# Thirteen tiles of v read as float by SyncE, and the second projection of two more groups by Strassen

## The chip, the core and the metric

The kernel runs on one core of a Trainium2 chip. A core has five engines with a queue of their own each: TensorE (PE: products; PEld: the weight load that precedes each), VectorE (DVE), ScalarE (ACT), GpSimd (POOL) and SyncE (SP), which here only issues DMAs. Sixteen DMA engines carry all transfers. The metric is the device time of one execution in microseconds.

## What is computed

Inputs q, k, v have the shape (4, 8, 768, 64): batch, heads, positions, head size. A recurrence over positions with a decay per head is followed by two projections with a sine activation between them.

```
gamma = 1.0 - 2.0 ** (-5.0 - np.arange(H, dtype=np.float32))
scale = 1.0 / np.sqrt(D)
for t in range(S):
    state = gamma[None, :, None, None] * state + np.einsum('bhd,bhe->bhde', k[:, :, t], v[:, :, t])
    y[:, :, t] = scale * np.einsum('bhd,bhde->bhe', q[:, :, t], state)
...
h = x @ w_in
s = np.sin(alpha * h)
g = h + s * s / (alpha + 1e-09)
return (g @ w_out).astype(np.float32)
```

x is y with the heads side by side: 3072 tokens of 512. w_in is 512 by 2048, w_out 2048 by 512, alpha has 2048 values.

## The kernel before

**Tiles and groups.** The 24 tiles of 128 tokens are taken in the order `P` (`order`): tiles 0 to 3 are the first of each batch, then come batch 0, batch 1, and batches 2 and 3 interleaved. A number n below means `P[n]`. Ten groups of 4, 2, 2, 2, 2, 2, 2, 2, 2 and 4 tiles pass through the projections: group 5 has tiles 12 and 13, group 6 tiles 14 and 15, group 7 tiles 16 and 17, group 8 tiles 18 and 19, group 9 tiles 20 to 23.

**Order of work.** The schedule is written by hand: each engine executes its instructions in the order in which the program emits them. `PLAN` is the order up to group 1. From group 2 on `phase(g, ...)` (L878) runs slots: a slot of a two-tile group makes two of the 16 blocks f of the hidden layer. It issues 8 products into `ph` (L610), the sine and the square on ScalarE (L613, L618), what is hung on the slot (`atts`: bursts of the recurrence, transposes, scalings), then its share of the second projection of the group before (`outs`), then `add` (L625, VectorE), which writes block f of `gT` and frees ph's bank of PSUM. What is in `behind_slot` comes last. "(7,1)" is slot 1 of group 7. Four banks of PSUM have the tag mm; ph and the outputs of the second projection share them.

**The second projection** of a group has 32 products of 512 columns for two tiles (`ff_out`, L634), with one copy per tile to SBUF on VectorE (L644) and one store by SyncE (L647). For the groups in `fast`, 8 and 9, it goes by Strassen (`Seven`): seven sums of eight products of 256 columns for each pair of tiles. Products 3 and 4 take blocks of gT as they are; products 5 and 2 take the sums "s", 7 and 6 the differences "d" and 1 the sums "x", which `mix_g` (L687) forms, in three operations for a slot's blocks, mostly on GpSimd (L710). The products' right sides are blocks of w_out or of sums of them, which `mix_w` forms (L675, L681): seven of ten pieces of 1024 elements on GpSimd, three on VectorE. `hold` copies product 5 and 2's bank b to SBUF, `cross`, `rest` and `main` (VectorE) make the outputs from banks a and c.

**Reads.** Tiles 0 to 10 are read one by one (`load_chunk`, into `qkr` and `vr`). The other 13 (batch 1's tiles 11 to 13, five of batch 2 and five of batch 3) are read "wide" by `load_seq` (L131, issue in L149): one DMA for each of the eight heads brings several tiles. All these are issued by GpSimd, and convert from float to bf16 on the way. GpSimd's queue has, after `PLAN`, q, k and v of batch 1, q, k and v of batch 2 and the first two tiles of batch 3's q and k, one directly behind the other; v and the other three tiles of batch 3 follow at (5,5) (`last_loads`). v is then multiplied in place by a table of decays (`scale_v`, L185): tiles 9 to 14 on VectorE at (2,3) to (4,6), the later ones on GpSimd. q and k are transposed by SyncE's DMA (`turn`, L297), each tile two bursts ahead; SyncE's queue holds these and the stores of the outputs in one order.

**Buffers that matter.** `gT` has one tag with two buffers of the largest size, 16 KB per partition, whatever the size of the group. `vr` has 11 buffers, `qkr` 10. w_mix lies in five buffers of qkr, in `dec` and in batch 1's `qk_seq1` once these are free; g_mix of group 8 in five of qkr, of group 9 in `qk_seq2` and `qk_seq3`.

Of the kernel before, what the change touches and what calls it, by code (L numbers as in the profile page):

```python
# [8 lines left out]
F32 = mybir.dt.float32  # L9
# [29 lines left out]
def kernel(  # L39
# [90 lines left out]

    def load_seq(bt, names="qkv", part=slice(None), between=None):  # L131
# [8 lines left out]
        fs = slice(2 * (now[0] - cs[0]), 2 * (now[-1] - cs[0]) + 2)  # L140
        for name, src in (("q", q), ("k", k), ("v", v)):
            if name not in names:
                continue
            for n, (b, m, e) in enumerate(heads):
                if n == 3 and between is not None:
                    scale_v(between, nc.gpsimd)
                r, at = half(b), 2 * m + e
                o = tv[r, fs, at, :] if name == "v" else tqk[r, fs, "qk".index(name), at, :]
                nc.gpsimd.dma_start(out=o, in_=src[bt, head(b, m, e), now[0] * C:(now[-1] + 1) * C, :].rearrange("(f i) d -> i f d", i=64))  # L149
# [35 lines left out]
    def scale_v(j, eng):  # L185
        t, by = raw["v", j], kg
        if wide(j):
            t, by = t.rearrange("i f p d -> i (f p) d"), kgq
        eng.tensor_mul(t, t, by[:, j % NCH, :, None].to_broadcast([128, H, D]))  # L189

# [405 lines left out]
    class Slot:  # L596


        def __init__(self, g, f, cols=None, nf=1, tag="mm"):
# [3 lines left out]
            if g not in gT:  # L603
                gT[g] = work.tile([128, FF, n], BF16, name="gT", tag="gT", bufs=2)
            w = self.hi - self.lo
# [46 lines left out]

    fast = (8, 9)
    FH, NH = FF // 2, d_model // 2
# [4 lines left out]
    def w_block(k, n, js):  # L659
# [3 lines left out]
             6: ((0, 0), (0, 1), ALU.add), 7: ((1, 0), (1, 1), ALU.add)}  # L663
    w_todo = [(n, i) for n in (4, 3, 1, 7, 6) for i in range(2)]

    def w_homes():
        for _ in range(5):
            yield big.tile([128, 4, NH], BF16, name="w_mix", tag="qkr", bufs=10)
        for pool, tag, n in ((consts, "dec", 2), (big, "qk_seq1", 3)):
            t = pool.tile([128, n, 4, NH], BF16, name="w_mix", tag=tag)  # L670
            for i in range(n):
                yield t[:, i]
    w_home = w_homes()

    def mix_w(eng):  # L675

        n, i = w_todo.pop(0)
        a, b, op = W_MIX[n]
        js = slice(4 * i, 4 * i + 4)
        w_mix[n, i] = next(w_home)  # L680
        eng.tensor_tensor(w_mix[n, i], w_block(*a, js), w_block(*b, js), op=op)  # L681

# [37 lines left out]
    class Seven:  # L720
# [20 lines left out]
        def right(self, n, j):  # L741
            if n in (5, 2):
                return w_out[:, j + FH * (n == 5), NH * (n == 5):NH * (n == 5) + NH]
            return w_mix[n, j // 4][:, j % 4]

# [26 lines left out]
        def store_both(self, o, n):  # L772

            t0, t1 = groups[self.g][2 * self.p:2 * self.p + 2]
            if self.g < NG - 1:
                self.store(0, o[:, 0], n)
                self.store(1, o[:, 1], 1 - n)
                return
# [19 lines left out]
        def main(self, which=None):  # L798
# [28 lines left out]
    def fast_pieces(g):  # L827
        J = range(FH)

        def banks(k):  # L830
            if k == "c":
                return psum.tile([128, 2, 512], F32, name="c", tag="pa")[:, 0, 0:NH]
            if "ab" not in po:
                po["ab"] = psum.tile([128, 2, 512], F32, name="ab", tag="two")
            return po["ab"][:, "ab".index(k)].rearrange("p (x n) -> p x n", x=2)
        s = Seven(g, 0, banks)
        return s.pieces((4, J), (3, J), (5, J), (2, J), lambda: s.hold(nc.vector), s.cross, (1, J), s.rest, (7, J), (6, J), s.main)
# [40 lines left out]
    def phase(g, outs, att, nf=1, on_vector=(), tags={}, early=()):  # L878


        no, done = len(outs), 0
        for n in range(FF // nf):
# [162 lines left out]

    load_seq(1, "q", between=P[8])
    load_seq(1, "k")
    load_chunk(P[10], "v")
    load_seq(1, "v")
    load_seq(2, "q")  # L1050
    load_seq(2, "k")
    load_seq(2, "v")
    load_seq(3, "q", slice(0, 2))
    load_seq(3, "k", slice(0, 2))
    for j in P[15:17] + P[18:19]:
        scale_v(j, nc.gpsimd)

# [12 lines left out]
    def B(old, new, first, beside, second):  # L1070

        return lambda: burst(old, new, first, beside=beside, second=second)

    for n in range(9, 17):
# [3 lines left out]
        at(where[n] if n < 16 else (5, 5), X(P[n + 2]))  # L1078
    for i, spot in ((16, (6, 4)), (18, (7, 4)), (20, (8, 1))):
# [6 lines left out]
    for i, spot in ((19, (6, 1)), (20, (6, 5)), (21, (7, 1)), (22, (7, 5)), (23, (8, 0))):  # L1086
        at(spot, X(P[i]))
    for i, spot in ((19, (6, 2)), (20, (6, 6)), (21, (7, 2)), (22, (7, 6)), (23, (8, 2))):
# [12 lines left out]
    for i, spot in ((9, (2, 3)), (10, (3, 0)), (11, (3, 3)), (12, (3, 7)), (13, (4, 3)), (14, (4, 6))):  # L1101
# [45 lines left out]
```

## Time and profile before

| | us |
|---|---|
| median of three runs | 205.69 (205.63 to 206.04) |
| the profiled execution | 207.02 |
| its span on the core | 205.2 |
| granted TensorE clock, mean | 0.997 |

The span runs from the first to the last instruction of the profile. Engine times are busy times; a matmul's end is modelled, so neighbouring rows of TensorE overlap by some tenths, and starts tell the pace. A group row gives operation, shapes, count, busy time, the mean of one and what ended the idle time before it. The chain of waits names, from the last instruction backwards, what each step waited for.

### The profile page before, as it was taken

How to read it: one execution, taken by the hardware profiler on the slowest of the kernel's cores; microseconds unless marked ns; L12 is line 12 of the kernel's file. 1: busy time of each engine (PE TensorE's matmuls, PEld its weight loads, DVE VectorE, ACT ScalarE, POOL GpSimd, SP SyncE). 2: the span in 40 equal slices, each digit the busy share in tenths (PEclk: the TensorE clock that was granted, in tenths of full speed). 3: DMA queues.
4: the chain of work that ended last, by engine and by line, in shares of the span. 5: the costliest groups of instructions: out<-in, count | busy, mean ns of one | idle time of the engine just before them, and what ended most of it. 6: DMA issues, size and time to landing. Idle time of an engine off the chain costs nothing.

```text
span 205.2 us, 6029 instructions
## 1 busy us (share of the span) xinstructions
PE 195.2 (95%) x2426; PEld 131.4 (64%) x2455; DVE 161.5 (79%) x344; ACT 151.8 (74%) x312; POOL 163.2 (80%) x204
## 2 busy tenths in 40 slices
PE   7889999999998999999999999999999999999993
PEld 7444544557765667666666676666766665555983
DVE  5787499877998887887998885995998775577853
ACT  7678888656996877877877959588586869999120
POOL 8998996999999996997399997999193876997000
PEclk9999999999999999999999999999999999999998
DMA  8999999999999999999996796994406101001123
GB/s 133 147 175 192 201 201 176 167 134 106 231 151 188 104 171 194 170 136 150 143 116 117 89 141 117 120 131 104 105 2 107 51 5 51 3 0 51 54 102 102
DMA packets 103580, 24.82 MB, mean 121 GB/s; under 512 B 93392, under 2 KB 101248, under 8 KB 103552
## 3 DMA queue, kind: packets, MB, share of 16 engines
q0 software_dynamic: 80080, 13.38, 92.8%
q1 hardware_dynamic: 23472, 11.06, 26.8%
q8 instruction: 19, 0.31, 0.7%
q14 instruction: 9, 0.07, 0.1%
HBM read 27.30 MB, written 6.29 MB: 164 GB/s over the span
## 4 chain that ended last, share of the span: by engine, by line
PE 83%; DMA 7%; POOL 4%; issue 2%; DVE 2%; ACT 1%; POOLq 0%
PE ph L610 37%; PE po L634 28%; DMA qkT<-qkr 4%; PE a L756 3%; DMA qkr<-in_q_dram 3%; PE ab L756 3%; POOL qkr L125 2%; PE b L756 2%; PE py L373 1%; POOL vr L125 1%; PE c L756 1%; PE pt L291 1%; PE pa L388 1%; PE py L437 1%; POOL w_in L161 1%
## 5 line engine op out<-in xcount | busy, mean ns | idle before, releaser
L625 DVE SCALAR_TENSOR_TENSOR gT<-s,rec_alpha,ph 128x256 bf16<-128x256 f32 (+3 forms) x164 | 79.4, 522 | 25.1 <-ACT s L618 24.6
L610 PE MATMUL ph<-xT,w_in 128*128 128x256 bf16 (+3 forms) x653 | 98.0, 291 | 0.3
L613 ACT ACTIVATE s<-ph,alpha_sb 128x256 f32<-128x256 f32 (+3 forms) x164 | 75.9, 505 | 28.1 <-PE ph L610 26.3
L610 PEld LDWEIGHTS <-w_in 128*128 128x128 bf16 x656 | 63.1, 98 | 29.6 <-DVE s_f L568 0.7
L634 PE MATMUL po<-w_out,gT 128*128 128x512 bf16 x264 | 70.3, 379 | 2.3 <-issue 1.9
L618 ACT ACTIVATE s<-s 128x512 f32<-128x512 f32 (+1 forms) x94 | 58.7, 626 | 2.8
L634 PEld LDWEIGHTS <-gT 128*128 128x128 bf16 x288 | 26.4, 98 | 20.8 <-DVE gT L625 0.5
L710 POOL TENSOR_TENSOR g_mix<-gT 128x512 bf16<-128x512 bf16 (+1 forms) x27 | 25.9, 994 | 7.2 <-DVE gT L625 7.2
L149 POOL DMA_DIRECT2D qk_seq<-in_q_dram x32 | 21.5, 712 | 6.6 <-DMA v_seq<-in_v_dram 6.1
L149 POOL DMA_DIRECT2D qk_seq<-in_k_dram x32 | 21.3, 720 | 1.5 <-DMA qk_seq<-in_q_dram 1.4
L149 POOL DMA_DIRECT2D v_seq<-in_v_dram x24 | 16.8, 743 | 0.0
L681 POOL TENSOR_TENSOR w_mix<-w_out 128x1024 bf16<-128x1024 bf16 x7 | 15.2, 2190 | 0.0
L756 PEld LDWEIGHTS <-g_mix 128*128 128x128 bf16 x128 | 11.9, 98 | 3.6
L644 DVE COPY o_sb<-po 128x512 f32<-128x512 f32 x15 | 10.3, 687 | 2.0 <-PE po L634 1.6
L125 POOL DMA_DIRECT2D vr<-in_v_dram x11 | 10.3, 932 | 1.2 <-DMA w_in<-in_moe_w_in_dram 0.7
L189 POOL TENSOR_TENSOR v_seq<-v_seq,kgq 128x512 bf16<-128x512 bf16 x9 | 9.8, 1097 | 1.4 <-DMA v_seq<-in_v_dram 1.4
L407 DVE TENSOR_TENSOR aTw<-pa,maskq 128x768 bf16<-128x768 f32 x10 | 9.5, 954 | 0.0
L495 DVE TENSOR_TENSOR xT<-py,qg 128x512 bf16<-128x512 f32 x13 | 8.9, 683 | 0.5 <-PE py L453 0.5
L869 PE MATMUL spare<-warm 128*128 128x112 bf16 (+1 forms) x52 | 7.9, 325 | 1.4 <-DVE warm L199 1.2
L391 DVE TENSOR_TENSOR aT<-pa,mask 128x1024 bf16<-128x1024 f32 x7 | 8.5, 1219 | 0.4 <-PE pa L388 0.4
L520 ACT CAST s_q<-s_f 128x256 bf16<-128x256 f32 x13 | 5.1, 393 | 2.7 <-DVE s_f L515 2.7
L165 POOL DMA_DIRECT2D w_out<-in_moe_w_out_dram x8 | 5.8, 727 | 1.2 <-DMA w_in<-in_moe_w_in_dram 0.8
(138 smaller groups left out, 217.7 us busy)
## 6 DMA issues: line engine op xcount, KB each, us to landing
out_dram<-o_sb SPq DMA_DIRECT2D x21, 256.0 KB, 3.9
w_in<-in_moe_w_in_dram POOLq DMA_DIRECT2D x8, 256.0 KB, 8.3
w_out<-in_moe_w_out_dram POOLq DMA_DIRECT2D x8, 256.0 KB, 7.9
vr<-in_v_dram POOLq DMA_DIRECT2D x11, 128.0 KB, 5.3
v_seq<-in_v_dram POOLq DMA_DIRECT2D x16, 80.0 KB, 4.7
qkr<-in_q_dram POOLq DMA_DIRECT2D x7, 128.0 KB, 6.4
qkr<-in_k_dram POOLq DMA_DIRECT2D x7, 128.0 KB, 5.8
qk_seq<-in_q_dram POOLq DMA_DIRECT2D x16, 48.0 KB, 4.4
```

Source lines behind the costliest of these rows:

```text
L125: nc.gpsimd.dma_start(out=t, in_=chunk_of(src, j))
L149: nc.gpsimd.dma_start(out=o, in_=src[bt, head(b, m, e), now[0] * C:(now[-1] + 1) * C, :].rearrange("(f i) d -> i f d", i=64))
L189: eng.tensor_mul(t, t, by[:, j % NCH, :, None].to_broadcast([128, H, D]))
L610: nc.tensor.matmul(self.ph[:, m, :], w_in[:, i, f * 128:(f + 1) * 128], xT[g][:, i, self.lo:self.hi], start=(m == 0 and i == 0), stop=(i = ...
L613: nc.scalar.activation(out=self.s[:, m, :], in_=self.ph[:, m, :], func=ACTF.Sin, scale=alpha_sb[:, f:f + 1])
L618: nc.scalar.activation(out=self.s, in_=self.s, func=ACTF.Square)
L625: nc.vector.scalar_tensor_tensor(gT[self.g][:, f, self.lo:self.hi], self.s[:, m, :], rec_alpha[:, f:f + 1], self.ph[:, m, :], op0=ALU.mult ...
L634: nc.tensor.matmul(po[g, ts], gT[g][:, f, ts * C:(ts + 1) * C], w_out[:, f, :], start=(f == 0), stop=(f == FF - 1))
L644: nc.vector.tensor_copy(o_sb, po[g, ts])
L681: eng.tensor_tensor(w_mix[n, i], w_block(*a, js), w_block(*b, js), op=op)
L710: eng.tensor_tensor(o, i0, i1, op=op)
L756: nc.tensor.matmul(t, self.left(n, j), r, start=k not in self.begun, stop=(j == FH - 1), skip_group_check=True)
```

## The change

In words:
- v of the 13 wide tiles is read by SyncE as float, without conversion, into a new tile `vf` of 16 pieces by 256 values; `scale_v` reads `vf` and writes bf16 into `v_seq`. Batch 1 takes pieces 0 to 5 of `vf`, batch 2 pieces 6 to 15, batch 3 pieces 0 to 9.
- `vf` shares the tag gA, with one buffer, with gT of the four-tile groups 0 and 9. gT of the two-tile groups keeps the tag gT with two, now smaller, buffers.
- `fast` is now 6, 7, 8 and 9. Group 6's pair is laid out over group 7's slots as 4, 5, 2 and hold, 3 and cross, nothing at the pair of the recurrence, 7, half of 6 and 1, the rest; its bank a is of tag mm, b and c of tag two. Group 7's is laid out over group 8's slots with a, b and c of tag mm.
- All w_mix sums are GpSimd's: ten pieces of 512 elements in freed buffers of vr, two of 1024 in dec, three in qk_seq1. g_mix of groups 6, 7 and 8 lies in qkr.
- GpSimd's queue is laid out anew from the end of `PLAN` on: between the wide reads of q and k stand mix_w and the scale_v of tiles 10 to 13, then those of tiles 14 to 18 and 20 at (3,4), (4,0) and (5,3); mix_g of groups 6 and 7 follows in their slots. VectorE keeps the scale_v of tile 9.
- SyncE reads v of batch 1 at (2,2), of batch 2 at (3,3), of batch 3 at (4,6).

```diff
-            for n, (b, m, e) in enumerate(heads):
-                if n == 3 and between is not None:
-                    scale_v(between, nc.gpsimd)
+            if name == "v":
+                vf = raw["vf"][:, 6:16] if bt == 2 else raw["vf"][:, 0:nh]
+                for i, c in enumerate(cs):
+                    raw["vf", bt * NCH + c] = vf[:, 2 * i:2 * i + 2]
+            for n, (b, m, e) in list(enumerate(heads))[some]:
+                if n in between:
+                    between[n]()
...
-                nc.gpsimd.dma_start(out=o, in_=src[bt, head(b, m, e), now[0] * C:(now[-1] + 1) * C, :].rearrange("(f i) d -> i f d", i=64))
+                o = vf[r, fs, at, :] if name == "v" else tqk[r, fs, "qk".index(name), at, :]
+                (nc.sync if name == "v" else nc.gpsimd).dma_start(out=o, in_=src[bt, head(b, m, e), now[0] * C:(now[-1] + 1) * C, :].rearrange("(f i) d -> i f d", i=64))
...
-    fast = (8, 9)
+    fast = (6, 7, 8, 9)
...
+    w_todo = {"vr": [(n, j, 2) for n in (7, 6) for j in range(0, FH, 2)] + [(1, 4, 2), (1, 6, 2)],
+              "dec": [(4, 0, 4), (4, 4, 4)], "seq": [(3, 0, 4), (3, 4, 4), (1, 0, 4)]}
...
+        if g == NG - 3:
+            s = Seven(g, 0, lambda k: psum.tile([128, 2, NH], F32, name=k, tag="mm", bufs=4)[:, slice(0, 2) if k != "c" else 0])
+            parts = [[(4, range(7))], [(4, range(7, FH)), (3, range(6))], [(3, range(6, FH)), (5, range(5))],
+                     [(5, range(5, FH)), (2, range(4))], [(2, range(4, FH)), s.hold], [s.cross, (1, J)], [s.rest, (7, J)],
+                     [(6, J), s.main]]
+            return [s.steps(*p) for p in parts]
+        if g < NG - 3:
...
+            parts = [[(4, J)], [(5, J)], [(2, J), s.hold], [(3, J), s.cross], [], [(7, J)], [(6, range(4)), (1, range(4))],
+                     [(1, range(4, FH)), s.rest, (6, range(4, FH)), s.main]]
+            return [s.steps(*p) for p in parts]
...
+            if g - 1 in fast and n == 5:
+                run(more, "exit1")
...
     def last_loads():
-        mix_w(nc.gpsimd)
         nc.gpsimd.tensor_copy(seen, st["qkT", P[17]][:, 0, 0:1])
-        load_seq(3, "v")
-        mix_w(nc.gpsimd)
-        mix_w(nc.gpsimd)
-        scale_v(P[17], nc.gpsimd)
-        load_seq(3, "qk", slice(2, None))
+        load_seq(3, "q", slice(2, None))
+        load_seq(3, "k", slice(2, None))
...
+    def loads():
+        load_seq(1, "v")
+        turn(P[12])
+        pieces_w(2, "vr")()
+        scale_v(P[10], nc.gpsimd)
+        pieces_w(2, "vr")()
+        load_seq(2, "q")
+        scale_v(P[11], nc.gpsimd)
+        load_seq(2, "k", between={4: scaled(P[12])})
+        scale_v(P[13], nc.gpsimd)
+        load_seq(3, "q", slice(0, 2), between={4: lambda: mix_w(nc.gpsimd, "dec")})
+        mix_w(nc.gpsimd, "dec")
+
+    at((2, 2), loads)
...
+    at((3, 3), lambda: load_seq(2, "v"))
+    at((4, 6), lambda: load_seq(3, "v"))
+    for spot, fn in (((3, 2), pieces_w(2, "vr")), ((3, 2), lambda: load_seq(3, "k", slice(0, 2), some=slice(0, 4))),
+                     ((3, 2), pieces_w(1, "vr")), ((3, 2), lambda: load_seq(3, "k", slice(0, 2), some=slice(4, 8))),
+                     ((3, 4), scaled(P[14], P[15])), ((3, 4), pieces_w(2, "vr")), ((4, 0), scaled(P[16], P[18], P[20])),
+                     ((4, 5), pieces_w(3, "seq")), ((4, 5), pieces_w(1, "vr")), ((5, 3), scaled(P[17]))):
+        mixes(spot, fn)
+    for g in (6, 7, 8):
+        for m in range(0, FH, 2):
+            mixes((g, m + 1), lambda g=g, m=m: mix_g(g, m, 2, nc.gpsimd))
```

More of the change, by code (lines that the diff above doesn't have):

```diff
@@ L140, in load_seq @@
         fs = slice(2 * (now[0] - cs[0]), 2 * (now[-1] - cs[0]) + 2)
+        if "v" in names and "vf" not in raw:
+            raw["vf"] = work.tile([128, 16, NP, D], F32, name="vf", tag="gA", bufs=1)
         for name, src in (("q", q), ("k", k), ("v", v)):
@@ L186, in scale_v @@
         t, by = raw["v", j], kg
+        o = t
         if wide(j):
-            t, by = t.rearrange("i f p d -> i (f p) d"), kgq
-        eng.tensor_mul(t, t, by[:, j % NCH, :, None].to_broadcast([128, H, D]))
+            o, t = (x.rearrange("i f p d -> i (f p) d") for x in (t, raw["vf", j]))
+            by = kgq
+        eng.tensor_mul(o, t, by[:, j % NCH, :, None].to_broadcast([128, H, D]))
     tok = consts.tile([128, NCH, 2], F32, name="tok")
@@ L603, in __init__ @@
             if g not in gT:
-                gT[g] = work.tile([128, FF, n], BF16, name="gT", tag="gT", bufs=2)
+                gT[g] = work.tile([128, FF, n], BF16, name="gT", tag="gA" if sizes[g] == 4 else "gT", bufs=1 if sizes[g] == 4 else 2)
             w = self.hi - self.lo
@@ L663, with mix_w @@
              6: ((0, 0), (0, 1), ALU.add), 7: ((1, 0), (1, 1), ALU.add)}
[L664 to L677, printed above, removed]
-        a, b, op = W_MIX[n]
-        js = slice(4 * i, 4 * i + 4)
-        w_mix[n, i] = next(w_home)
-        eng.tensor_tensor(w_mix[n, i], w_block(*a, js), w_block(*b, js), op=op)
+    w_todo = {"vr": [(n, j, 2) for n in (7, 6) for j in range(0, FH, 2)] + [(1, 4, 2), (1, 6, 2)],
+              "dec": [(4, 0, 4), (4, 4, 4)], "seq": [(3, 0, 4), (3, 4, 4), (1, 0, 4)]}
+    w_home = {}
+    def mix_w(eng, home):
+        n, i, c = w_todo[home].pop(0)
+        a, b, op = W_MIX[n]
+        if home == "vr":
+            to = big.tile([128, 2, NH], BF16, name="w_mix", tag="vr", bufs=11)
+        else:
+            if home not in w_home:
+                w_home[home] = (consts if home == "dec" else big).tile(
+                    [128, 2 if home == "dec" else 3, 4, NH], BF16, name="w_mix", tag="dec" if home == "dec" else "qk_seq1")
+            to = w_home[home][:, (2 if home == "dec" else 3) - 1 - len(w_todo[home])]
+        eng.tensor_tensor(to, w_block(*a, slice(i, i + c)), w_block(*b, slice(i, i + c)), op=op)
+        for j in range(c):
+            w_mix[n, i + j] = to[:, j]
     def blocks(t, first, *dims):
@@ L743, in right @@
                 return w_out[:, j + FH * (n == 5), NH * (n == 5):NH * (n == 5) + NH]
-            return w_mix[n, j // 4][:, j % 4]
+            return w_mix[n, j]
         def mm(self, n, j, half=None):
@@ L810, in main, with steps @@
                 self.store(1, self.o[:, 1, c], 1, c.start, c.stop)
+        def steps(self, *parts):
+            return [fn for part in parts for fn in ([part] if callable(part) else self.pieces(part))]
         def pieces(self, *parts):
@@ L835, in banks, with between @@
             return po["ab"][:, "ab".index(k)].rearrange("p (x n) -> p x n", x=2)
+        if g == NG - 3:
[5 more added lines that the diff above has]
+        if g < NG - 3:
+            def between(k):
+                if k == "a":
+                    return psum.tile([128, 2, NH], F32, name=k, tag="mm", bufs=4)
+                return psum.tile([128, 2, 512], F32, name=k, tag="two")[:, 0].rearrange("p (x n) -> p x n", x=2)[:, slice(0, 2) if k == "b" else 0]
+            s = Seven(g, 0, between)
+            parts = [[(4, J)], [(5, J)], [(2, J), s.hold], [(3, J), s.cross], [], [(7, J)], [(6, range(4)), (1, range(4))],
+                     [(1, range(4, FH)), s.rest, (6, range(4, FH)), s.main]]
+            return [s.steps(*p) for p in parts]
         s = Seven(g, 0, banks)
@@ L878, in phase @@
     def phase(g, outs, att, nf=1, on_vector=(), tags={}, early=()):
-        no, done = len(outs), 0
+        plan = outs if outs and isinstance(outs[0], list) else None
+        no, done = 0 if plan else len(outs), 0
         for n in range(FF // nf):
@@ L901, in phase @@
                 rest[0] = fresh
+            for fn in plan[n] if plan else ():
+                fn()
             while done < min(no, no * (n + 1) * nf // FF):
@@ L1044, with scaled @@
         act(word)
-    load_seq(1, "q", between=P[8])
+    def scaled(*js):
+        return lambda: [scale_v(j, nc.gpsimd) for j in js]
+    load_seq(1, "q", between={3: scaled(P[8])})
     load_seq(1, "k")
     load_chunk(P[10], "v")
[L1049 to L1056, printed above, removed]
     where = {}
@@ L1072, in B, with pieces_w @@
         return lambda: burst(old, new, first, beside=beside, second=second)
+    def pieces_w(n, home):
+        return lambda: [mix_w(nc.gpsimd, home) for _ in range(n)]
     for n in range(9, 17):
@@ L1077 @@
         at(where[n], B(P[n - 1], new, first, P[17] if n == 16 else None, e3 if n == 15 else None))
-        at(where[n] if n < 16 else (5, 5), X(P[n + 2]))
+        if n != 10:
+            at(where[n] if n < 16 else (5, 5), X(P[n + 2]))
     for i, spot in ((16, (6, 4)), (18, (7, 4)), (20, (8, 1))):
```

15 lines of the change are left out of this document (4 added, 11 removed).

## The prediction

> **What bounds the kernel now.** Read first the page's busy shares and its chain that ended last, then the busy time by stage: 62.3 to 122.2 us, then groups 6, 7, 8 and 9.
>
> ```profile
> span 205.2 us, 6029 instructions
> ...
> PE 195.2 (95%) x2426; PEld 131.4 (64%) x2455; DVE 161.5 (79%) x344; ACT 151.8 (74%) x312; POOL 163.2 (80%) x204
> ...
> PE 83%; DMA 7%; POOL 4%; issue 2%; DVE 2%; ACT 1%; POOLq 0%
> ```
>
> ```profile
> 62.30:122.20 59.90, 58.58 (x812) 40.73 (x822) 51.70 (x107) 45.36 (x98) 51.55 (x71) 1.00 1.71 143
> 122.20:137.60 15.40, 15.29 (x207) 10.48 (x208) 13.01 (x29) 12.29 (x27) 13.99 (x20) 1.00 1.33 123
> 137.60:152.90 15.30, 15.19 (x207) 10.52 (x208) 12.04 (x27) 11.75 (x25) 10.77 (x10) 1.00 0.43 77
> 152.90:169.70 16.80, 16.23 (x253) 11.30 (x256) 12.88 (x27) 12.22 (x27) 11.21 (x11) 1.00 0.24 50
> 169.70:189.80 20.10, 20.00 (x121) 11.88 (x122) 13.82 (x21) 19.37 (x33) 17.45 (x19) 1.00 0.08 27
> ```
>
> After span come PE, PEld, DVE, ACT, POOL, clock, DMA share and GB/s. TensorE has 0.1 us idle in all of group 6 and 0.1 in all of group 7. So each product removed in group 7 or 8 is worth its time, and each microsecond that TensorE must wait is paid in full: nothing behind it has slack to give back (group 9 runs TensorE at 20.00 of 20.10 us and ScalarE at 19.37). GpSimd has 1.4 us left in group 6 and 4.5 in group 7, and the change adds to just these.
>
> **What the Strassen pairs remove.** The chain of waits, first in group 6, then at the end, shows the rates:
>
> ```profile
> 134.31 0.87 PE ph L610 x8
> 135.19 0.86 PE po L634 x4
> ...
> 197.70 1.75 PE a L756 x16
> ```
>
> A 512-column output product costs 0.86 / 4 = 0.215 us, a 256-column one 1.75 / 16 = 0.109. A pair now takes 32 of the first, 6.88 us; by Strassen 56 of the second, 6.10. With 0.78 to 0.86 a pair I take 0.86 (proportion to columns: 8 x 0.87 / 8), so groups 6 and 7 together give **-1.7 us**.
>
> The Trainium skill, "TensorE: Matmul & The Clock Gate", section "Back-to-back issue gap", speaks against it: in a stream of weight load and product pairs it has 81 ns for 128 columns and 131 for 512. Estimated from that page, 98 ns for 256 would make a Strassen pair 5.5 us against 4.2, +2.6 us for the two and 208.3 in all; this trace has 0.215 us for 512 columns, not 0.131, and here the measurement decides.
>
> VectorE gets cross, rest and main (three operations) for two copies, and ScalarE one hold:
>
> ```profile
> L644 DVE COPY o_sb<-po 128x512 f32<-128x512 f32 x15 | 10.3, 687 | 2.0 <-PE po L634 1.6 <-ACT o_sb L642 0.4
> L765 ACT COPY b_sb<-b 128x512 f32<-128x512 f32 x2 | 1.2, 585 | 5.2 <-PE b L756 5.2
> ```
>
> That is +0.7 us of VectorE and +0.6 of ScalarE a pair, beside 12.04 and 11.75 of 15.3 us (group 7): hidden by that slack. Of rest and main only main ends a group, where the copy of the second tile stands today. In group 8 two output banks are held out of the four tagged mm, so ph has two. A ph starts at 137.62, and the add of the ph before it, which starts 1.74 earlier, ends at 138.50 + 0.87 = 139.37. So a bank is held for 3.49 us, and two slots are 3.48:
>
> ```profile
> 137.62 1.04 PE L610 MATMUL ph<-xT,w_in 128*128 128x256 bf16 x8
> ...
> 139.36 1.04 PE L610 MATMUL ph<-xT,w_in 128*128 128x256 bf16 x8
> ...
> 145.54 0.42 PE L544 MATMUL y<-qkT,s_q 64*64 64x128 bf16 x16
> ```
> ```profile
> 138.50 0.87 DVE L625 SCALAR_TENSOR_TENSOR gT<-s,rec_alpha,ph 128x256 bf16<-128x256 f32 x2
> ```
>
> So ph is just in time; the bursts between stretch the slots. I take 0, at worst 0.5. At (7,0), that is group 7's slot 0 at 137.62 (y of (7,4) at 145.54 fixes the count), product 4 of group 6 needs block f=15, whose add ends at 138.50 + 0.87 = 139.37, while TensorE is there at 137.62 + 0.87 + 7 x 0.109 = 139.25: **+0.15** with the signal.
>
> **What decides: GpSimd up to (7,1).** There TensorE wants product 5 of group 6 for all eight blocks. Its left side is the sum "s" of g_mix; blocks 6 and 7 come from the last mix_g of group 6, on GpSimd, behind all its earlier work in one queue. TensorE reaches block 6 at 139.36 + 0.87 + 6 x 0.109 + 0.15 = 141.0. When is GpSimd there? Its rows before:
>
> ```profile
> 67.28 0.91 POOL L125 DMA_DIRECT2D vr<-in_v_dram  x1 [0.17 <-issue]
> 68.17 3.97 POOL L149 DMA_DIRECT2D v_seq<-in_v_dram  x6
> ...
> 79.24 2.13 POOL L149 DMA_DIRECT2D qk_seq<-in_q_dram  x3 [2.04 <-DMA v_seq<-in_v_dram]
> 81.34 4.30 POOL L149 DMA_DIRECT2D qk_seq<-in_k_dram  x6
> ...
> 102.61 4.28 POOL L149 DMA_DIRECT2D qk_seq<-in_k_dram  x7 [0.51 <-DMA qk_seq<-in_q_dram]
> ...
> 107.88 3.05 POOL L189 TENSOR_TENSOR v_seq<-v_seq,kgq 128x512 bf16<-128x512 bf16 x3
> 110.89 2.12 POOL L681 TENSOR_TENSOR w_mix<-w_out 128x1024 bf16<-128x1024 bf16 x1
> ...
> 126.06 5.31 POOL L149 DMA_DIRECT2D qk_seq<-in_q_dram  x8
> 131.28 5.35 POOL L149 DMA_DIRECT2D qk_seq<-in_k_dram  x8
> 136.47 1.22 POOL L189 TENSOR_TENSOR v_seq<-v_seq,kgq 128x512 bf16<-128x512 bf16 x1
> 137.47 0.78 POOL L577 CAST s_q<-s_f 128x512 bf16<-128x512 f32 x1
> ```
> ```profile
> L149 POOL DMA_DIRECT2D qk_seq<-in_q_dram x32 | 21.5, 712 | 6.6 <-DMA v_seq<-in_v_dram 6.1 <-DMA vr<-in_v_dram 0.3
> L149 POOL DMA_DIRECT2D qk_seq<-in_k_dram x32 | 21.3, 720 | 1.5 <-DMA qk_seq<-in_q_dram 1.4
> L149 POOL DMA_DIRECT2D v_seq<-in_v_dram x24 | 16.8, 743 | 0.0
> ...
> L253 POOL TENSOR_TENSOR qg<-qg,step 128x512 f32<-128x512 f32 x5 | 5.1, 1044 | 0.1
> ...
> vr<-in_v_dram POOLq DMA_DIRECT2D x1, 128.0 KB, 3.5
> ...
> 158.22 2.90 POOL L710 TENSOR_TENSOR g_mix<-gT 128x512 bf16<-128x512 bf16 x3 [3.52 <-DVE gT L625]
> ```
>
> Up to 68.17 the queue is unchanged. Then, until the last wide read is issued, it holds in the new order (starts apart, from these rows):
> - 16 reads of batch 2 at 0.70 (79.24 to 81.34 for three): 11.2
> - 16 of batch 3's first two tiles at 0.61: 9.8
> - 16 of its last three at 0.65 (126.06 to 136.47): 10.4
> - scale_v of tiles 10 to 18 and 20, ten at 1.0: 10.0. Five of them and more were VectorE's or came later. That they read float is not in the trace; the nearest rows (qg, float in and out, 1044 ns; bf16 as above, 1.02) leave 1.0 to 1.1.
> - five mix_w of 1024 elements at 2.12: 10.6, and ten of 512 at 1.07 (half; a slot's mix_g, 512 + 512 + 256 elements in 2.90, would give 1.16): 10.7. VectorE had three of the ten large ones.
> - the tiny copy 0.2, and 0.6 of waiting for tile 10's v, issued at 67.28 (its kind lands in 3.5 us in this stretch).
>
> Sum 63.5, so the reads end at 131.7 (now 136.47: the 24 issues of v, 16.8 us, and most of the 8.1 us of waits before reads go; 12 of mix_w and 6 of scale_v come). Then, in order: mix_g 2.9, scale_v 1.0, mix_g 2.9, the copy of s_q 0.6, mix_g 2.9 and the first operation of the fourth, 1.15 (2.90 x 512 / 1280): 11.5, and s is there at **143.2**. TensorE is there at 141.0: it stands 2.2 us, if GpSimd meets no wait on a read at all. Behind the waiting product stand all of TensorE's products, and behind those ScalarE and VectorE.
>
> ```profile
> qkT<-qk_seq SPq DMA_TRANSPOSE x13, 6.2
> ```
>
> The waits for v go with v, but reads issued beside DMA transposes land late (a transpose itself takes 6.2 us at the median), and GpSimd waits, by the pattern of these rows, for the eighth read before each. Between reads there is now other work, so most waits vanish: of 0 to 3 us I take 0.7. The lag is **+2.9**, bounds 1.0 (mix_w and scale_v, 31 us, 4% quicker) to 5.2.
>
> **SyncE.** It issues 24 reads of v. The trace's nearest reads with pieces of 256 bytes are the first two of q and k, at 0.46 and 0.56 us:
>
> ```profile
> L172 SPq DMA_DIRECT2D o_sb<-in_q_dram x1: 457/457/457, 0.7 to 0.7; - x1
> ```
> ```profile
> 69.16 1.23 SPq L297 DMA_TRANSPOSE qkT<-qk_seq  x1
> ...
> 110.36 1.74 SPq L297 DMA_TRANSPOSE qkT<-qk_seq  x1
> ...
> 109.46 0.30 PE L421 MATMUL pa<-v_seq,qk_seq 64*64 64x64 bf16 x16
> ...
> 118.10 0.23 PE L395 MATMUL pb<-qkT 64*64 64x128 bf16 x4
> ```
>
> Batch 1's follow the transpose of tile 11 (69.16) and land near 79, where tile 11's scale_v comes (79.6): even. Batch 3's overwrite what tiles 14 and 15 leave, so SyncE waits there for GpSimd's scale_v of tile 15 (about 108); the store and the transpose of tile 17 stand behind eight issues, so it starts at 112 to 113 instead of 110.36 and lands at 116 to 119; TensorE wants it at 118.10. Cost 0 to 3, taken 0: it would come out of the same lag, since a later TensorE finds GpSimd further on. VectorE loses five scale_v (3.4 us, tiles 10 to 14) and three mix_w in stages that TensorE sets: 0. Tile 14's v is scaled at about 106 and wanted at 109.46: 0 while GpSimd is under 3 us late.
>
> **Sum.** -1.7 + 0.15 + 2.9 = +1.3 us on the profiled execution's span of 205.2 (it took 207.02 with the profiler). The median of the runs is 205.69; I put the same difference on it: **207.0 us**.
>
> **Rivals.**
> - *GpSimd is on time.* If the reads end by about 130.5 or the small operations run quicker, s is there within 1 us of TensorE and the pairs give their 1.7: 205.69 - 1.55 = 204.1, at the edge 205.2. It decides at a lag of 1.55, s at 142.6. For it: the sum has an error of a microsecond on 75. Against it: nearly every term is a measured start-to-start, and waits only add.
> - *A wash:* lag 1.2 to 2.0, 205.3 to 206.1.
> - *Reads stay slow.* If v's packets on the other queue hold back q's and k's, a good third of the 8.1 us that GpSimd waits today stays, 3 us: lag 5.2, 205.69 - 1.55 + 5.2 = 209.3. For it: DMA share 1.71 in this stretch. The Trainium skill, "DMA: Bandwidth & Descriptors", section "Rules for kernel authors", has that spreading transfers over issuing engines saves issue time only, all running on the same 16 engines; by it this rival would be likelier than I make it, and the trace, which has v on one queue only, cannot tell.
> - *256-column products lose more than they save* (+2.6, 208.3): against it stand the 1.75 us for 16.
>
> **Chances.** Forecast with lag 2.0 to 4.6 (206.1 to 208.7): 0.40. On time: 0.33. Wash: 0.15. Slow reads: 0.10. Wide products: 0.02. A measurement of this kernel tells about 0.2%, 0.4 us, from no change. Faster 0.33, same 0.15, slower 0.52. The likeliest case's own range is 206.1 to 208.7; the range that should hold the time 8 times in 10 reaches to the on-time case: 204.0 to 208.9.
>
> **What would show it.** Right: in the changed kernel's waits TensorE or its weight load waits for GpSimd's g_mix between group 7's slots 1 and 2, 2 to 4 us, its only stretch there; GpSimd is busy without a break from 68 to 145; the last wide read is issued near 131 to 133. Groups 7 and 8 hold 112 products of 0.109 us for 64 of 0.215. Wrong: g_mix of group 6 ends before 141.5, and TensorE shows no gap; or the gap lies at (5,6) before tile 17's scores (SyncE), or in group 8 before ph (banks).

## The result and the profile after

The changed kernel takes 214.57 us (median of four runs, 213.67 to 215.45); the kernel before, run beside it on the same chip, 205.87. The ratio is 1.041, 95% interval 1.036 to 1.047: 8.7 us slower. The prediction was 207.0, its range ended at 208.9.

The page of the changed kernel, with the busy shares and the chain that ended last:

```profile
span 212.5 us, 6178 instructions
...
PE 196.8 (93%) x2479; PEld 136.8 (64%) x2503; DVE 158.3 (75%) x338; ACT 152.6 (72%) x314; POOL 181.2 (85%) x217
...
PE 58%; POOL 20%; DMA 7%; DVE 4%; SPq 3%; ACT 3%; issue 3%; POOLq 0%; ACTq 0%
```

TensorE's share of the chain fell from 83 to 58%, and GpSimd's rose from 4 to 20%. TensorE now stands, that is, it does nothing because what its next product needs is not there. The view of waits says for what (total, times, longest):

```profile
PEld L403 <- DMA qkT<-qk_seq: 6.4, 2, 4.7
...
PE pa L403 <- DMA qkT<-qk_seq: 4.6, 1, 4.6
...
PE pb L403 <- DMA qkT<-qk_seq: 1.5, 1, 1.5
...
PEld L764 <- POOL g_mix L718: 0.9, 1, 0.9
```

Two waits for a transpose, 4.6 us at (4,5) (tile 14's scores) and 1.5 at (5,6) (tile 17's); the wait for GpSimd at (7,1), which the prediction made the only one, is 0.9 for the weight load. The first has a sequel. In the table of stretches (after the span: PE, PEld, DVE, ACT and POOL busy, granted clock, DMA share, GB/s) the stand, and what follows it:

```profile
100.20:104.90 4.70, 0.12 (x12) 0.06 (x8) 0.47 (x2) 1.27 (x3) 4.69 (x5) 1.00 1.43 219
104.90:108.50 3.60, 3.27 (x49) 2.05 (x51) 3.10 (x7) 0.00 (x0) 3.60 (x6) 0.53 1.36 244
```

After 4.6 us without work the granted clock is 0.53 for 3.6 us: TensorE is 91% busy there and does little more than half the work, 1.7 us lost. Counted from ph to ph, the slot with the first stand and the one behind it took 6.3 us more than before, the slot at (5,6) 1.7 more, group 7's phase 1.3 more (16.57 for 15.30) and group 8's 0.55 less (16.26 for 16.81). In front of these the change was 1.3 ahead, mostly because the 1.14 us that the profiled run of before stood at 61.2 is not there. The sum is 7.4, against 7.3 between the spans.

SyncE's own queue shows what stands in front of the transposes, first tile 14's in the profile of before, then the change:

```profile
90.85 1.23 SPq L297 DMA_TRANSPOSE qkT<-qk_seq  x1
```
```profile
81.82 13.42 SPq L155 DMA_DIRECT2D vf<-in_v_dram  x8
...
99.81 1.76 SPq L305 DMA_TRANSPOSE qkT<-qk_seq  x1
...
112.79 6.69 SPq L155 DMA_DIRECT2D vf<-in_v_dram  x8
...
121.22 1.28 SPq L305 DMA_TRANSPOSE qkT<-qk_seq  x1
```

Tile 14's transpose starts at 99.81 (90.85 before), tile 17's at 121.22 (110.36). Batch 2's eight reads of v take 13.4 us to issue, 1.7 each, where the prediction had 0.46 to 0.56. Both things can have delayed the transpose: the queue it stands in, and the k that it transposes. The view of DMA issues in the ten microseconds from 80 on (KB of one, median us from issue to landing), before and then after:

```profile
DMA packets 10283, 1.67 MB, mean 167 GB/s; under 512 B 10154, under 2 KB 10154, under 8 KB 10282
...
qk_seq<-in_k_dram POOLq DMA_DIRECT2D x8, 80.0 KB, 4.4
```
```profile
DMA packets 7222, 1.72 MB, mean 172 GB/s; under 512 B 6965, under 2 KB 6965, under 8 KB 7221
...
vf<-in_v_dram SPq DMA_DIRECT2D x6, 160.0 KB, 10.2
qk_seq<-in_k_dram POOLq DMA_DIRECT2D x8, 80.0 KB, 10.4
```

The same eight reads of k land in 10.4 us instead of 4.4, beside reads of v that the view counts at twice the bytes each, since v stays float. All transfers together move as much as before, 172 GB/s for 167.

### The profile page after: what moved, and what is told of

Same layout as the page of the kernel before. It is cut to its first block, busy times and chain, and to the rows that moved or that the text cites. A ratio compares the mean times of both kernels' runs of the same rounds, so it can differ in the third digit from the quotient of the medians.

```text
span 212.5 us, 6178 instructions
## 1 busy us (share of the span) xinstructions
PE 196.8 (93%) x2479; PEld 136.8 (64%) x2503; DVE 158.3 (75%) x338; ACT 152.6 (72%) x314; POOL 181.2 (85%) x217
## 4 chain that ended last, share of the span: by engine, by line
PE 58%; POOL 20%; DMA 7%; DVE 4%; SPq 3%; ACT 3%; issue 3%; POOLq 0%; ACTq 0%
PE ph L618 27%; PE po L642 14%; POOL qk_seq L155 7%; PE a L764 5%; POOL g_mix L718 5%; DMA w_out<-in_moe_w_out_dram 3%; SPq L155 2%; POOL qkr L125 2%; PE ab L764 2%; DMA vf<-in_v_dram 2%; PE b L764 2%; POOL vr L125 2%; PE c L764 2%; DMA out_dram<-o_sb 2%; ACT s L621 2%
## 5 line engine op out<-in xcount | busy, mean ns | idle before, releaser
L642 PE MATMUL po<-w_out,gT 128*128 128x512 bf16 x206 | 55.5, 383 | 2.2 <-issue 1.8
L718 POOL TENSOR_TENSOR g_mix<-gT 128x512 bf16<-128x512 bf16 (+1 forms) x51 | 48.9, 992 | 5.0 <-DVE gT L633 3.5
L642 PEld LDWEIGHTS <-gT 128*128 128x128 bf16 x224 | 20.7, 98 | 16.8 <-issue 0.5
L764 PEld LDWEIGHTS <-g_mix 128*128 128x128 bf16 x208 | 19.4, 98 | 5.9 <-POOL g_mix L718 0.9
L687 POOL TENSOR_TENSOR w_mix<-w_out 128x512 bf16<-128x512 bf16 (+1 forms) x15 | 22.0, 1496 | 0.0
L197 POOL TENSOR_TENSOR v_seq<-vf,kgq 128x512 bf16<-128x512 f32 x13 | 13.6, 1061 | 1.2 <-DMA vf<-in_v_dram 1.2
L764 PEld LDWEIGHTS <-gT 128*128 128x128 bf16 x88 | 7.9, 98 | 2.2 <-DVE gT L633 0.3
L764 PE MATMUL b<-w_out,g_mix 128*128 128x256 bf16 x64 | 8.5, 273 | 0.6 <-POOL g_mix L718 0.6
L652 DVE COPY o_sb<-po 128x512 f32<-128x512 f32 x11 | 7.6, 690 | 2.0 <-PE po L642 1.6
L764 PE MATMUL a<-w_mix,gT 128*128 128x256 bf16 (+1 forms) x72 | 8.7, 261 | 0.0
```

The costliest lines, as they stand in the source:

```text
L197: eng.tensor_mul(o, t, by[:, j % NCH, :, None].to_broadcast([128, H, D]))
L642: nc.tensor.matmul(po[g, ts], gT[g][:, f, ts * C:(ts + 1) * C], w_out[:, f, :], start=(f == 0), stop=(f == FF - 1))
L687: eng.tensor_tensor(to, w_block(*a, slice(i, i + c)), w_block(*b, slice(i, i + c)), op=op)
L718: eng.tensor_tensor(o, i0, i1, op=op)
L764: nc.tensor.matmul(t, self.left(n, j), r, start=k not in self.begun, stop=(j == FH - 1), skip_group_check=True)
```

## The experiments

Each is the changed kernel with the edit that is named. A time without an interval is one run, and the four runs of the change lie between 213.67 and 215.45; the kernel before, on the same chips, had medians of 205.8 to 207.1.

**v behind the transposes that it held up.** First batch 2's v alone, moved from (3,3) to (3,6); in both runs GpSimd's scalings of tiles 14 and 15 and two pieces of w_mix move with it, from (3,4) to (3,7):

```diff
-    at((3, 3), lambda: load_seq(2, "v"))
+    at((3, 6), lambda: load_seq(2, "v"))
```

> The change, but SyncE reads batch 2's v at (3,6), behind the transpose of tile 14, and not at (3,3), ahead of it. Theory A (sharing): in the change batch 2's v and batch 2's k are carried at the same time, so the last k lands 10.4 us after its issue instead of 3.8, and tile 14's transpose waits for that. Theory B (queue): the transpose waits because SyncE needs 13.4 us for the eight issues ahead of it. Both expect that the transpose starts near 91 to 93 instead of 99.8, that TensorE's 4.6 us before (4,5)'s scores and the 3.4 us at half clock behind them go, and some 5 to 6 us of the time: 208 to 210. Only A expects that the last k of batch 2 then lands about 4 to 5 us after its issue. If less than 2 us go, both fall.

Then batch 3's as well, from (4,6) to (5,2):

> As the first, and SyncE reads batch 3's v at (5,2), behind the transpose of tile 17, and not at (4,6), ahead of it. Theory A and B: the 1.55 us of TensorE before tile 17's scores at (5,6) go as well, so this is 1.5 to 1.8 us faster than the first: 206.5 to 208.5. TensorE then reaches group 7 some 7 us earlier than in the change, and its wait for GpSimd's g_mix at (7,1) grows from 0.6 us to 2 to 5.

214.16 and 213.47 us: two misses in time. The waits of the first, then of the second run:

```profile
PE pb L403 <- DMA qkT<-qk_seq: 3.8, 1, 3.8
...
PE pa L403 <- DMA qkT<-qk_seq: 1.6, 1, 1.6
```
```profile
PE pa L403 <- DMA qkT<-qk_seq: 2.6, 1, 2.6
...
PE b L764 <- POOL g_mix L718: 2.6, 2, 2.4
```

The reads of k land in 7.2 and 7.5 us and tile 14's transpose starts at 95.8 and 95.2, where 91 to 93 was expected. The 4.6 at (4,5) goes in both and comes back: in the first as 1.6 at (5,1), where tile 15's transpose now stands behind the reads, and 3.8 instead of 1.5 at (5,6); in the second as 2.6 at (5,1) and 2.6 at (7,1). The stand at (5,1) is new with the edit; those at (5,6) and (7,1) had been hidden in part behind the first. Less than 2 us went, so by the expectation's own words both theories fell: these two runs leave it open what delayed the transpose.

**Another queue for batch 2's v.** ScalarE issues it, at the same place, so that SyncE's queue is free.

```diff
-                (nc.sync if name == "v" else nc.gpsimd).dma_start
+                ((nc.scalar if bt == 2 else nc.sync) if name == "v" else nc.gpsimd).dma_start
```

The arguments of `dma_start` are the same in both lines.

> The change, but ScalarE's queue issues batch 2's v, at the same place (3,3). SyncE's queue is free for tile 14's transpose. Theory A (sharing): the last k of batch 2 still lands 8 us or more after its issue, near 97 to 99, and the transpose starts only then. Theory B (queue): k lands near 91 and the transpose starts there, 7 us earlier than in the change. The time itself says little, since ScalarE stands for the eight issues, 5 to 13 us.

218.79 us. SyncE's row for tile 14's transpose, and the DMA issues from 80 to 90 us:

```profile
99.58 1.23 SPq L305 DMA_TRANSPOSE qkT<-qk_seq  x1
```
```profile
vf<-in_v_dram ACTq DMA_DIRECT2D x5, 160.0 KB, 10.9
qk_seq<-in_k_dram POOLq DMA_DIRECT2D x8, 80.0 KB, 9.8
```

SyncE had nothing in front of that transpose after 83.2, and it still starts at 99.58 (99.81): it waits for k, which lands as late as in the change. So the delay does not need SyncE's queue (which in the change is free again at 98.6). That the reads of v hold back the reads of k is measured further down, by the runs without these reads. The Trainium skill, "DMA: Bandwidth & Descriptors", section "Issuing engines are not separate DMA queues", has that whichever engine starts a DMA, it runs on the same 16 engines and interleaves with the others. The 9.8 and 10.4 us agree. The time of this run says nothing more, since ScalarE stood in its issues and TensorE behind it for 11.3 us.

**The reads without the pairs.** `fast = (8, 9)`, no g_mix for groups 6 and 7.

> The change, but with groups 8 and 9 alone by Strassen, as before: the reads, the scale_v and the mix_w of the change stay, the mix_g of groups 6 and 7 go. If the reads alone cost what the change lost, this takes as long as the change or up to 1.5 us less or more: 213 to 216, with the same wait of 4.6 us at (4,5). If the pairs of groups 6 and 7 bring their 1.7 us net, it is slower than the change by as much; if they bring nothing, the two agree.

214.76 us, with stands of 5.1 at (4,5) and 1.1 at (5,6): the reads and the new order of GpSimd's queue cost all that the change costs without the two pairs.

**Batch 2's v later still, or by GpSimd.** First at (4,2), behind tile 15's transpose, with batch 3's at (5,2) and the scalings of tiles 14 to 16, 18 and 20 moved to (4,2) and (4,4); then issued by GpSimd right behind batch 2's k, with tiles 14 and 15 scaled and three w_mix pieces formed by VectorE.

> The change with batch 2's v issued by SyncE behind tile 15's transpose, at (4,2) in place of (3,3), and batch 3's v behind tile 17's, at (5,2) in place of (4,6); the scalings that read them follow later in GpSimd's queue. Theory A (what costs is a transpose that stands behind or beside the reads of v): both tile 14's and tile 15's transposes land before TensorE wants them, no stand of over 0.5 us at (4,5) and at (5,6); v itself lands near 109 to 110 and is scaled by 111.5 to 112.5, so that a stand of 1.5 to 2.5 us is left at (5,1), now on GpSimd's scaling; 210 to 212 us in all with the lag at (7,1) of about 2.4 us. Theory C (the reads of v cost their time wherever they stand, since the sum of packets is too large for the stretch): a stand of over 3 us at (5,1) or a new one at (4,5); 213 us or more.

> The change with batch 2's v issued by GpSimd directly behind batch 2's k, still as float into vf; batch 3's v by SyncE at (5,2); tiles 14 and 15 scaled by VectorE and the three pieces of w_mix in qk_seq1 formed by VectorE, so that GpSimd's queue has 2.7 us less in all (5.6 us of issues for 6.3 of w_mix and 2.1 of scaling). Theory A (sharing of the engines delays k): k of batch 2 lands within 6 us, tile 14's transpose starts before 95.5, no stand at (4,5), (5,1) or (5,6) of over 0.5 us, and no stretch at half clock; the lag at (7,1) falls from 2.4 to under 1 us; 205.0 to 206.3 us. Theory C (float reads cost too many packets in this stretch on any queue): a stand of 2 us or more at (4,5) or (5,1); 209 us or more.

218.15 us, and a ratio of 1.076 (1.069 to 1.083). The waits of the first, then of the second:

```profile
POOL v_seq L197 <- DMA vf<-in_v_dram: 4.8, 1, 4.8
...
PE b L764 <- POOL g_mix L718: 3.4, 2, 2.4
```
```profile
POOL v_seq L197 <- DMA vf<-in_v_dram: 9.0, 1, 9.0
...
PE b L764 <- POOL g_mix L718: 6.9, 3, 3.0
```

In the first, v itself is late (5.1 us of TensorE at (5,1)); in the second, GpSimd waits 9.0 us in order for batch 3's v, and what stands behind it in its queue, g_mix too, is late; a wait of 2.3 for a transpose is left at (4,5). The sums I expected were wrong in both: moving a read later moved the wait, from SyncE's transposes to GpSimd's scalings.

**Without the reads.** Batch 2's tiles, then batch 2's and 3's, are scaled from the first two pieces of vf, and their v is not read, so their output is not the reference's.

```diff
-                    raw["vf", bt * NCH + c] = vf[:, 2 * i:2 * i + 2]
+                    raw["vf", bt * NCH + c] = raw["vf"][:, 0:2] if bt in (2, 3) else vf[:, 2 * i:2 * i + 2]
+                if bt in (2, 3):
+                    continue
```

> The change without the reads of batch 2's v: its five tiles are scaled from the first two pieces of vf, so their part of the output is not the reference's. Theory A (batch 2's v on SyncE holds back batch 2's k and with it tile 14's transpose): k's last read lands within 6 us, the stand at (4,5) is gone and with it the stretch at half clock; what is left is batch 3's v (1 to 4 us at (5,6)) and GpSimd at (7,1) (2 to 3 us): 210 to 212.5 us. Rival (the new order of GpSimd's queue alone is late with k): k lands over 8 us after its issue without the reads of v too, the stand at (4,5) stays at 3 us or more, 213.5 us or more.

> The change without the reads of batch 2's and of batch 3's v (their tiles are scaled from the first two pieces of vf). Theory A: no stand at (4,5), (5,1) or (5,6) and no half clock; left are the pairs (about 0.5 us gained), GpSimd's lag at (7,1), some 2 to 3 us as the prediction had it, and the 0.7 of the empty slot: 206.5 to 208.5 us, which is the predicted time; all that the result has above it is then the reads of v. Rival (GpSimd's lag is worse than forecast by itself, its w_mix at 2.1 and waits on q and k): a stand of over 4 us at (7,1), 209 us or more.

219.13 and 214.42 us, the second as long as the change itself. The first lost the stand at (4,5) and has one of 8.65 at (5,6): batch 3's v must wait there for more scalings than in the change, since all of batch 2's now read the pieces that it overwrites. That part is the edit's own doing, and the run shows only that k lands in 7.4 us and (4,5) is clear without batch 2's v. The second has, for the reads of k issued from 80 to 90 us and for tile 14's transpose:

```profile
qk_seq<-in_k_dram POOLq DMA_DIRECT2D x8, 80.0 KB, 6.3
```
```profile
95.31 1.23 SPq L307 DMA_TRANSPOSE qkT<-qk_seq  x1
```

In all four runs that have batch 2's v in flight beside k, on SyncE's or ScalarE's queue, k lands in 8.2 to 10.4 us and the transpose starts at 99.6 to 101.0; in the eight others with this order of reads k lands in 5.8 to 7.5 and the transpose starts at 93.1 to 97.6. So the reads of v do hold back k. By this run, they make 4.5 of the 9.0 us by which the transpose starts later in the change (99.81 for 90.85). The other 4.5 come with the new order of GpSimd's queue: it has issued the last of these reads at 90.4 instead of 87.4, and they land in 6.3 us instead of 4.4. Alone, this makes no stand at (4,5). No other transpose holds TensorE up either, and its timeline (start, length) shows at (7,1):

```profile
140.63 0.60 PE L766 MATMUL b<-w_out,g_mix 128*128 128x256 bf16 x4
143.33 0.39 PE L766 MATMUL b<-w_out,g_mix 128*128 128x256 bf16 x2 [2.10 <-POOL g_mix L720]
146.15 0.61 PE L766 MATMUL b<-w_out,g_mix 128*128 128x256 bf16 x2 [2.42 <-POOL g_mix L720]
```
```profile
146.20:149.70 3.50, 3.50 (x17) 2.43 (x18) 0.00 (x0) 1.17 (x3) 3.50 (x4) 0.50 0.00 0
```

With TensorE on time, GpSimd's sums for product 5 make it wait 4.5 us, as the rival had it, and the half clock follows here too (the second view above; it reaches to 151, about 2.5 us lost). GpSimd's last rows before those sums:

```profile
129.54 5.36 POOL L157 DMA_DIRECT2D qk_seq<-in_k_dram  x8
134.74 3.06 POOL L720 TENSOR_TENSOR g_mix<-gT 128x512 bf16<-128x512 bf16 x3
```

**GpSimd's queue made shorter.** The three sums w_mix in qk_seq1, 6.3 us of GpSimd, are left out (products 3 and half of 1 take blocks of w_out as they are), so that the output is not the reference's, first with both reads left out, then with all reads in place; and, third, the kernel without reads of batch 2's and 3's v and without the pairs of groups 6 and 7.

```diff
         a, b, op = W_MIX[n]
+        if home == "seq":
+            for j in range(c):
+                w_mix[n, i + j] = w_block(*a, slice(i + j, i + j + 1))[:, 0]
+            return
```

> The change without the reads of batch 2's and 3's v and without the three sums w_mix in qk_seq1 (products 3 and half of 1 take blocks of w_out as they are): GpSimd's queue is some 6.3 us shorter. Theory D (two bounds side by side: the reads of v hold TensorE up at (4,5) and (5,6), and GpSimd's queue alone holds it up by as much at (7,1), so that taking away one leaves the other): no stand over 0.7 us anywhere, no half clock, 205.5 to 207.5 us, 7 us less than the run that has only the reads left out. Rival (what is left lies in the pairs themselves, in groups 7 and 8): 210 us or more with no stand at (7,1).

> The change with all its reads, without the three sums w_mix in qk_seq1. Theory D: the stands at (4,5) and (5,6) stay as they are (4.6 and 1.6 us, with the half clock), the 0.6 at (7,1) goes: 213.5 to 214.5 us; so 6.3 us taken from GpSimd bring 1 us at most, while the reads are there. Rival (GpSimd's queue delays the reads, and so all stands): they go with it, under 211 us.

> The change's order of GpSimd's queue without the two more pairs and without the reads of batch 2's and 3's v. Theory D: neither bound is there, since nothing waits for g_mix at (7,1): no stand of over 0.7 us, 205.5 to 207 us, level with before; with the reads (run before) it was 214.8, with the pairs 214.4, with both 214.6. Rival (the new order costs by itself, w_mix and scalings on GpSimd slowing others): 209 us or more.

205.46, 213.57 and 209.28 us. The first two came out as theory D had them, the first 0.04 us under its range. The third misses by 2.3 us and lies in the rival's range. It has no stand from (4,1) on, as expected, but was 2.25 us behind the profile of before at that point, by a later start of group 2's slots (48.8 us for 47.1; 46.7 to 48.1 in the other runs with this order) and 1.2 us for an early transpose (0.7 in one other run). One run cannot tell whether the new order costs that or this execution alone; the run of 205.46, with the same order, speaks against the order. The table puts them side by side (us):

| | v of batches 2 and 3 read | not read |
|---|---|---|
| pairs, all sums (with the reads: the change) | 214.57 | 214.42 |
| pairs, three sums w_mix left out | 213.57 | 205.46 |
| no pairs in groups 6 and 7 | 214.76 | 209.28 |

Leaving out the reads alone brings 0.15 us, the three sums alone 1.0, both within the spread of the change's own runs; leaving out both brings 9.1. The change has two bounds side by side, the reads up to (5,6) and GpSimd's queue up to (7,1), of nearly the same size.

**What the pairs are worth.** In the run of 205.46 us nothing stands in groups 7 and 8 but the one row below. Its stretches for group 7's and group 8's phase, then TensorE's row:

```profile
136.20:151.98 15.78, 14.99 (x234) 12.82 (x232) 12.12 (x28) 12.15 (x26) 12.84 (x15) 1.00 0.41 68
151.98:168.24 16.26, 16.12 (x283) 13.63 (x280) 13.92 (x28) 12.73 (x28) 14.56 (x16) 1.00 0.29 51
```
```profile
146.48 1.05 PE L620 MATMUL ph<-xT,w_in 128*128 128x256 bf16 x8 [0.71 <-DVE s_f L578]
```

Group 6's pair makes its phase 0.48 longer than before (15.30), group 7's makes its 0.55 shorter (16.81): together 0.07, not 1.7. Group 6's layout leaves slot 4 without output products, and slot 5's ph starts no sooner, since TensorE waits there for VectorE: that slot took 3.12, where before it took 3.14 with 0.86 of output products in it. Slot 0 took 1.92 for 1.74 (block f=15), slot 6 1.99 for 1.74. Filling slot 4 does not mend it. In the run below that does so, slot 4 takes 3.11 with six products in it; slots 5 and 7 get 0.2 shorter each, slot 6 0.4 longer, since product 1's bank c waits 0.73 for VectorE there, and the phase takes 15.77.

**The pairs with the reads of before.** The kernel before with its reads of v through GpSimd, and the pairs: both with the change's layout; both with slot 4 filled; both with product 1 last as well; then only group 7's, three times, the last two with sums w_mix moved to other slots. VectorE forms all w_mix here; in the runs with both pairs it also scales tile 17 and forms group 6's last g_mix.

> The kernel before with all its reads (v through GpSimd as bf16) and only the two more pairs by Strassen, with the change's layout over the slots; w_mix by VectorE, four tiles' reads untouched. If the pairs are worth what 256-column products say (0.86 us each) and only the empty slot of group 6's layout takes 0.7 us back: 1.0 us less than before, 0.993 to 0.997 of it. If the pairs bring nothing (rows of the change against the run without them: 0.5 us or less): 0.997 to 1.003. If GpSimd, which has the reads and group 6's sums, is late at (7,1) here too: a stand there of over 1 us and no gain.

> As the run with the pairs alone, with group 6's products 7, 6 and 1 moved up by up to one slot, so that slot 4 of group 7 is not empty of them. If the empty slot costs 0.7 us (TensorE reaches the next ph before VectorE has freed its bank): 0.7 us less than the run with the empty slot, 1.6 to 1.8 us less than before, ratio 0.991 to 0.994. If that stand is the recurrence's and not the empty slot's, it stays: no difference between the two.

> As the run with the pairs alone and slot 4 filled, with the sums w_mix one a slot, away from GpSimd's three scalings, and group 6's product 1 last, so that its bank c is wanted half a slot later. If what the runs with the pairs alone lost before group 6 (1.5 us in front of slot (5,4) and 0.8 at the tenth tile) was VectorE held up by GpSimd, that is gone, and so is the 0.73 before c: 1.0 to 1.6 us less than before, ratio 0.992 to 0.996. If it was VectorE's added work itself: no gain over before, 1.000 to 1.010.

> The kernel before with its reads and only group 7's pair added to Strassen, w_mix by VectorE in one piece a slot while GpSimd issues reads. If that pair brings what group 8's phase showed in the runs (16.3 for 16.8 us): 0.5 us less than before, ratio 0.996 to 0.999. If VectorE's added sums are held up again by GpSimd's operations (2.76 us for one in the run with the pairs alone, 0.68 before): a stand near them and 1.000 to 1.005.

> As the run with only group 7's pair added, with the sums w_mix on VectorE moved out of (5,0) to (5,2), where one took 2.63 us beside GpSimd's three scalings (0.42 elsewhere) and TensorE then stood 1.95 us. If that stand was all that this run lost: 2 to 2.8 us less than it, 0.989 to 0.996 of before. If VectorE's added work there only moves: 0.998 to 1.004.

> As the last run with only group 7's pair added, with the one sum w_mix that still stood beside a scaling of GpSimd's (2.76 us at (6,5), TensorE stood 1.35 behind it) moved to (5,5), where GpSimd only issues reads. If those 1.35 us were all that the pair had lost: 1.0 to 1.5 us less than the last run, ratio to before 0.993 to 0.998. If another sum is caught in its place: 0.999 to 1.004.

| kernel before with | ratio to before | 95% interval |
|---|---|---|
| both pairs | 1.013 | 1.009 to 1.017 |
| and slot 4 filled | 1.011 | 1.003 to 1.018 |
| and product 1 last, sums spread | 1.005 | 1.002 to 1.008 |
| group 7's pair alone | 1.005 | 1.000 to 1.009 |
| and sums away from (5,0) to (5,2) | 1.001 | 0.998 to 1.004 |
| and the last sum away from (6,5) | 0.999 | 0.996 to 1.001 |

No version beats the kernel before by more than its measurement can tell. The first missed all three of its ranges, the next four came out where no gain was expected, and the last, at 0.9986, lies between its two. Group 8's phase takes 16.25 in it too, so the 0.55 us that group 7's pair gains there may be real; it lies inside the interval. What the last two won back is one kind of stand, 1.95 and then 1.35 us. VectorE's and GpSimd's timelines of the last but one, and TensorE's row behind them:

```profile
135.43 2.76 DVE L679 TENSOR_TENSOR w_mix<-w_out 128x512 bf16<-128x512 bf16 x1
```
```profile
135.20 1.16 POOL L189 TENSOR_TENSOR v_seq<-v_seq,kgq 128x512 bf16<-128x512 bf16 x1
136.19 0.72 POOL L577 CAST s_q<-s_f 128x512 bf16<-128x512 f32 x1
136.77 1.14 POOL L189 TENSOR_TENSOR v_seq<-v_seq,kgq 128x512 bf16<-128x512 bf16 x1
```
```profile
139.03 0.81 PE L634 MATMUL po<-w_out,gT 128*128 128x512 bf16 x3 [1.35 <-DVE gT L625]
```

A sum that takes VectorE 0.42 us took 2.76, for as long as GpSimd had three operations without a break. In the last run no such sum lies beside GpSimd's operations, the longest of the 15 takes 0.87, and TensorE has no stand over 0.2 us from 40 us on. The Trainium skill, "SBUF — State Buffer", section "SBUF: two separate sides", has that VectorE, with two inputs from SBUF, and GpSimd lock one shared pair of ports for a whole instruction, and the other blocks; the 2.76 against 0.42 agrees, though the wait lasted for three of GpSimd's operations.

## Why the prediction was wrong

- **SyncE, "cost 0 to 3, taken 0": this step failed.** It worked out batch 1's and batch 3's v and not batch 2's, which held back k (10.4 us to land, 6.3 in the run without the reads, 4.4 before) and so tile 14's transpose: 4.6 us at (4,5), which goes without these reads. It priced the issues at 0.46 to 0.56; they took 0.7 to 1.7. Batch 3's v, forecast to start the transpose of tile 17 at 112 to 113, started it at 121.2: the scaling of tile 15, which it waits for, came 4.7 us later than the 108 taken, and eight issues took 6.7 instead of some 4. The rival "reads stay slow" named the cause, v's packets beside k's, but let it act on GpSimd's waits alone, at 209.3; it hit the transposes.
- **That a late transpose would come out of GpSimd's lag** was right, and worth more than I saw: the two do not add. With the reads in place TensorE stands 0.6 at (7,1); without them 4.5.
- **GpSimd's lag, +2.9 with bounds 1.0 to 5.2:** 4.9 in the run without the reads (146.15 against 141.23; TensorE stands for 4.5 of it), inside the bounds and 2.0 over the value. s was forecast for 143.2. The reads end at 134.74, not 131.7: it began 0.7 later, waited 2.4 on the way (0.6 in the sum, 0.7 beside it), and the sums of 512 elements came 1.11 apart instead of 1.07. From the last read to s it took 11.4, forecast 11.5. In the run where TensorE is on time this lag, with the half clock behind it, is the main loss, and the time is 214.4. The reason given for the waits, that reads beside transposes land late, holds in one stretch of the profile of before (8.7 us for q's from 91 to 97, with two transposes; 3.9 for k's from 102 to 107, with none) and not in another (2.5 for q's from 125 to 131, with two).
- **No term for the clock.** A stand was priced at its length; behind the 4.6 us in the change the half clock cost 1.7 more, behind the 4.5 in the run without the reads 2.5.
- **The pairs, -1.7:** 0.07 gained. The products do run at 0.109 us. Group 8's phase gave 0.55 of its 0.86 and group 7's lost its 0.86 and 0.48 more, mostly in the empty slot 4: there the time did not go with the work, since the next ph waited for VectorE. The +0.15 for block f=15 was right (0.18).
- **Banks in group 8, taken 0:** right, no stand there over 0.1. **VectorE and ScalarE, 0:** right in the change, where w_mix is GpSimd's, but for the 0.7 at slot 5 of group 7; in the kernels that gave it to VectorE it was not.
- **What would show it:** "the gap lies at (5,6) before tile 17's scores (SyncE)" is the sign of an error that did appear; the one at (4,5) was not on the list. The last wide read was issued at 137.2, not near 131 to 133.

## What to carry to other kernels

A read put on an idle queue was not free here: it took DMA time from what else was in flight. So price it by what lands later, and follow that to the first product that needs it. Before pricing a wait, work out every chain that meets the same engine: here two bounds of one size stood side by side, and each experiment that removed one found the other. Removing TensorE's work from a slot paid only where what the next instruction waits for was there by then.

## What the runs showed of the hardware

- Within or after stands of 3.8, 4.1, 4.6, 5.1, 8.7 and 11.3 us, after one of 2.6, and after two within 5 us, of 2.1 and 2.4 or of 1.0 and 2.4, TensorE's granted clock was 0.5 for a stretch of 3.4 us or more. After single stands of 1.6, 2.3 and 2.4 it stayed at 1.0, but after one of 1.7, nine us behind one of 2.3, it fell. So the runs show no length at which it begins. The stand of 4.6 us in the change cost 6.3.
- Reads of k (80 KB each) landed in a median of 8.2 to 10.4 us beside reads of v (160 KB each) that SyncE issued, 9.8 beside those that ScalarE issued, and 5.8 to 7.5 in the runs with batch 2's v later or not at all. SyncE's eight issues of v took 13.4 us beside the reads of k, 5.5 in another stretch of a run without them.
- Two sums of VectorE with two bf16 inputs, beside three operations of GpSimd without a break, took 2.76 and 2.63 us; elsewhere such a sum took 0.42.
